# Attention by chunks of keys: the left-over keys of two pairs of heads put into one chunk

## The chip, the cores and the metric

The kernel runs on one core of a Trainium2 chip. The metric is the device time of one execution in microseconds (us), the median of three runs. Engines are named as the profile names them: PE is TensorE (PEld its weight loads), DVE is VectorE, ACT is ScalarE, SP the queue that issues most DMAs.

## What is computed

The reference is attention with a sigmoid in place of the softmax, followed by two MLPs; all of it in float32. Cut to the attention, which is the part that the change touches:

```python
# q, k, v: (2, 12, 448, 64): 2 batches, 12 heads, 448 positions, 64 wide
scores = scale * np.matmul(q, k.transpose(0, 1, 3, 2)) - np.log(S)
attn = 1.0 / (1.0 + np.exp(-scores))
out = np.matmul(attn, v)
# then: rms norm, silu(x @ w_gate) * (x @ w_val) @ w_out, and silu(h @ w_in) @ w_out
```

No weight is normalised over the keys, so the keys can be taken in any grouping and the products with v are simply added up.

## The kernel before

The 12 heads of a batch are taken in 6 pairs, so there are 12 pairs in all (`pairs`, L328). Head 0 of a pair lies on partitions 0 to 63, head 1 on 64 to 127. The 448 keys of a pair are cut into `NC` = 4 chunks of `CP` = 112.

- `prep(i)` (L344) splits the keys and queries of pair i on DVE into a high part in float32r and the rest (`ks`).
- `scores(i, c)` (L361) computes the scores of one chunk for both heads, keys on the partitions of PSUM, 448 queries along the row. Three products (high by high, low by high, high by low) are summed, each for two heads: 6 matmuls in float32r (L366), each on 64 rows of the array and 112 columns; the two heads stand on different halves of the rows and write to different banks of PSUM (`ps[:, h]`). One ACT instruction (L374) turns both heads' scores into the weights `a`. Three such PSUM tiles `sc` exist.
- `attend(i, c)` (L377) multiplies the weights by the values: one float32 matmul per head (L382) on 112 rows and 64 columns, head 0 on the left half of the columns and head 1 on the right, summed over the four chunks in one PSUM tile `av`. There are two `av` tiles, for alternate pairs.
- `collect(i)` (L390) copies a finished `av` to SBUF on DVE (L395) and squares it on ACT (L398) for the norm; both must have read it before its buffer is used again.

The order is written out by hand in the loop at L499 to L525. The 48 chunks go in 16 batches of three. One turn of the loop issues, in this order: the `collect` of the pairs that the turn before finished, the three `scores` of a batch (with `prep` of the next pair and the loads of the pair after the next two where a pair begins), the `add_square` of the collected pairs, the three `attend` of the batch before, and then what `PLAN` lists for the turn: `w` is one step of preparing the first weights of the MLPs (ACT or DVE), `n` one step of the norm of batch 0 (`norm_first`; its two float32 matmuls are L411 and L448). Each engine takes its instructions in the order in which they were issued; waits on semaphores join the engines. SP issues the loads in order too: `kq` (keys and queries, 4 buffers), `vr` (values, 5 buffers) and `raw` (weights).

After the loop the MLPs follow, with an order made by a planner (`Plan`, L65). Its matmuls (L678, L726) are in float32r on the whole array, 448 columns of data each. The change does not touch the planner or its numbers.

Of the kernel before, what the change touches and what calls it, by code (L numbers as in the profile page):

```python
# [9 lines left out]
F32 = mybir.dt.float32  # L10
F32R = mybir.dt.float32r
# [3 lines left out]
AF = mybir.ActivationFunctionType  # L15
# [3 lines left out]
B, H, S, D = 2, 12, 448, 64  # L19
NP = H // 2  # L20
DM = H * D
FF1, FF2 = 1536, 2048
P = 128
CP = 112
NC = S // CP
KD, K1, K2 = DM // P, FF1 // P, FF2 // P
SLAB = 6 * P
HALF = 3 * P
# [10 lines left out]
BUSY_A = 3.2  # L39
ZO = True  # L40
LOADED = (6, 7)
PLAN = ",,ww,ww,ww,ww,ww,ww,ww,ww,wnn,wnn,wnn,wnn,wnn,wnn,nn".split(",")
LOADS = (0, 2)
VALS = (2, 3, 4, 5)
RING = 4
# [143 lines left out]
def tile_attention_two_mlps(  # L189
# [9 lines left out]
    nc = tc.nc  # L199
# [9 lines left out]
    def ps_tile(name):  # L209
        return psum[-1].tile([P, 2, 512], F32, tag="ps", name=name)  # L210
# [41 lines left out]
    def load_next():  # L252
        load(order.pop(0))
# [4 lines left out]
    def low(dst, src, hi):  # L258
        nc.vector.tensor_tensor(dst, src, hi.bitcast(F32), ALU.subtract)  # L259
# [47 lines left out]
    def step():  # L307
        do = next(steps, None)
        if do:
            do()  # L310
# [4 lines left out]
    logs = const.tile([P, 1], F32, name="logs")  # L315
# [5 lines left out]
    with ExitStack() as actx:  # L321
        ap = actx.enter_context(tc.tile_pool(name="ap", bufs=2))
        at = actx.enter_context(tc.tile_pool(name="at", bufs=8))
        pctx = ExitStack()
        psum = [pctx.enter_context(tc.tile_pool(name="scp", bufs=3, space=PSUM))]
        avp = pctx.enter_context(tc.tile_pool(name="avp", bufs=2, space=PSUM))

        pairs = [(b, hp) for b in range(B) for hp in range(NP)]  # L328
        kq, vr, ks, att, av, acc, sqs = {}, {}, {}, {}, {}, {}, {}

        def load_pair(i):
            b, hp = pairs[i]
            kq[i] = ap.tile([P, 2, S], F32, tag="kq", name=f"kq{i}", bufs=4)
            if i:
                nc.sync.dma_start(kq[i], kqd[b, hp])
            else:
                for j, queue in enumerate((nc.sync, nc.scalar)):
                    queue.dma_start(kq[i][:, j], kqd[b, hp, :, j])

        def load_v(i):  # L340
            vr[i] = ap.tile([CP, NC, 2, D], F32, tag="vr", name=f"vr{i}", bufs=5)
            nc.sync.dma_start(vr[i], vd[pairs[i]])

        def prep(i):  # L344

            raw = kq.pop(i)
            ks[i] = kst = ap.tile([P, 2, 2, S], F32R, tag="ks", name=f"ks{i}")
            if i:
                nc.vector.tensor_copy(kst[:, 0], raw)  # L349
                nc.vector.tensor_tensor(kst[:, 1], raw, kst[:, 0].bitcast(F32), ALU.subtract)  # L350
            else:
                (hk, hq), (lk, lq) = ([kst[:, j, n] for n in range(2)] for j in range(2))
                head_, tail = slice(0, CP), slice(CP, S)
                nc.vector.tensor_copy(hk[:, head_], raw[:, 0, head_])
                low(lk[:, head_], raw[:, 0, head_], hk[:, head_])
                nc.scalar.activation(hq, raw[:, 1], AF.Copy)  # L356
                low(lq, raw[:, 1], hq)
                nc.vector.tensor_copy(hk[:, tail], raw[:, 0, tail])
                low(lk[:, tail], raw[:, 0, tail], hk[:, tail])

        def scores(i, c):  # L361
            ps = ps_tile(f"sc{i}_{c}")
            for step, (jk, jq) in enumerate(((0, 0), (1, 0), (0, 1))):
                for h in range(2):
                    rows = slice(h * D, (h + 1) * D)
                    nc.tensor.matmul(  # L366
                        ps[:CP, h, :S],
                        ks[i][rows, jk, 0, c * CP : (c + 1) * CP],
                        ks[i][rows, jq, 1, :],
                        start=(step == 0),  # L370
                        stop=(step == 2),
                    )
            a = at.tile([CP, 2, S], F32, tag="a", name=f"a{i}_{c}")
            nc.scalar.activation(a, ps[:CP, :, :S], AF.Sigmoid, bias=logs[:CP], scale=D**-0.5)  # L374
            att[i, c] = a

        def attend(i, c):  # L377
            if c == 0:
                av[i] = avp.tile([P, 512], F32, tag="av", name=f"av{i}")
            ps, a = av[i][:, :S], att.pop((i, c))  # L380
            for h in range(2):
                nc.tensor.matmul(  # L382
                    ps[h * D : (h + 1) * D],
                    vr[i][:, c, h, :],
                    a[:, h, :],
                    start=(c == 0),
                    stop=(c == NC - 1),
                )

        def collect(i):  # L390

            b, hp = pairs[i]
            ps = av.pop(i)[:, :S]
            if i < SQUARED:
                nc.vector.tensor_copy(xr[hp // 2][:, b, hp % 2], ps)  # L395
            which, home_ = ("s1", sqs) if hp else ("s0", acc)
            sq = home_[i if hp else b] = sp.tile([P, S], F32, tag=which, name=f"{which}{i}")
            nc.scalar.activation(sq, ps, AF.Square)  # L398
            if i >= SQUARED:
                nc.vector.tensor_copy(xr[hp // 2][:, b, hp % 2], ps)  # L400

        def add_square(i):

            b, hp = pairs[i]
            if hp:
                nc.vector.tensor_tensor(acc[b], acc[b], sqs.pop(i), ALU.add)

        def square_sums(b, ps):

            for c in range(NC):  # L410
                nc.tensor.matmul(  # L411
                    ps[:CP, c : c + 1], acc[b][:, c * CP : (c + 1) * CP], ones[:, 0:1], start=True, stop=True
                )

        def rsqrt(b, ps):

            home = sp.tile([P, S], F32, tag="s2", name=f"rsqrt{b}")[:CP]
            ms, y, t = (home[:, n * NC : (n + 1) * NC] for n in range(3))
            nc.vector.tensor_scalar(ms, ps[:CP, :NC], 1.0 / DM, EPS, ALU.mult, ALU.add)
            nc.vector.tensor_scalar(t.bitcast(U32), ms.bitcast(U32), 1, None, ALU.logical_shift_right)  # L420
# [3 lines left out]
            for j in range(3):  # L424
# [4 lines left out]
                nc.vector.scalar_tensor_tensor(y, t, 1.5, y, ALU.add, ALU.mult)  # L429
            diag = sp.tile([P, S], F32, tag="s3", name=f"diag{b}")[:CP].rearrange("p (c u) -> p c u", c=NC)  # L430
            nc.vector.tensor_tensor(
# [46 lines left out]
        n = len(pairs)  # L478
# [17 lines left out]
        nc.vector.memset(ones, 1.0)  # L496
        prep(0)
        turn_, ready = 0, []
        chunks = [(i, c) for i in range(n) for c in range(NC)]  # L499
        batches = [chunks[j : j + BATCH] for j in range(0, len(chunks), BATCH)]  # L500
        for before, batch in zip([[]] + batches, batches + [[]]):
            for i in ready:
                collect(i)
            for i, c in batch:
                if c == 0:
                    if i + 1 < n:
                        prep(i + 1)
                    if i + 3 < n:
                        load_pair(i + 3)
                        load_v(i + 3)  # L510
                    if i in LOADS:
                        load_next()
                scores(i, c)
            while ready:
                add_square(ready.pop(0))
            for i, c in before:
                attend(i, c)
                if c == NC - 1:
                    ready.append(i)
            for what in PLAN[turn_]:  # L520
                if what == "w":
                    step()
                else:
                    next(normal, None)
            turn_ += 1  # L525
# [20 lines left out]
    def dve(n, fn, deps=(), **more):  # L546
        return plan.add("D", 0.071 + n / 960, fn, deps, **more)
# [12 lines left out]
    def new(tag, dtype, name, n=2):  # L560
        return pools[tag[0]].tile([P, n, 2, S], dtype, tag=tag, name=name)
# [447 lines left out]
    def opened_product(n, b):  # L1009
        banks = [lambda b_=b_: opened[n](b_) for b_ in range(2)]  # L1010
        return product(banks, range(6 * n, 6 * n + 6), xs, (b,), last=b == 1)
# [4 lines left out]
    q_ = plan.add("P", 0.45, lambda: square_sums(1, sums), ready=SQUARES)  # L1016
# [39 lines left out]
    f = [Whole(f"h{p}", f"F{p}", new(f"F{p}", F32, f"h{p}")) for p in range(K1 // 2)]  # L1056
    fdone = {}
    done0 = []
    for n in range(4):
        e = opened_product(n, 1)[-1]  # L1060
# [16 lines left out]
    for p in range(1, NP1):  # L1077
# [6 lines left out]
        else:  # L1084
# [11 lines left out]
            for m in range(2):  # L1096
                e = dve(NT, lambda m=m: tt(f[1]()[:, m], pv[m](), f[1]()[:, m], ALU.mult), [ends[m]] + silu)
# [44 lines left out]
    keys = [("h", k) for k in range(6, K1)]  # L1142
# [27 lines left out]
    for p in range(NP2):  # L1170
        if p == 0:
# [3 lines left out]
            for m in range(2):  # L1175
                ps = Banks(f"i{m}", True)
                tiles = range(6 * (s + m), 6 * (s + m) + 6)
                e = product([ps.bank(b) for b in range(2)], tiles, [("y", k) for k in range(KD)], (0, 1), take="ps", start=ps.start)[-1]
# [21 lines left out]
    keys = [("g", k) for k in range(6, K2)]  # L1200
# [75 lines left out]
```

## Time and profile before

| | us |
|---|---|
| median of three runs | 541.43 (541.39 to 541.68) |
| the profiled execution, its own time | 541.37 |
| its span, first to last instruction | 539.4 |
| busy in the span: PE / PEld | 534.2 (99%) / 462.2 (86%) |
| busy in the span: DVE / ACT | 407.7 (76%) / 332.9 (62%) |

A matmul line counts one instruction; a float32 matmul leaves two records in the trace, a float32r one leaves one. Two records on different parts of the array can run at the same time, so the busy time of a line is not the sum of its durations. The chain that ended last is read from the last instruction back to the first.

### The profile page before, as it was taken

The numbers are of one execution on the slowest core, as the hardware profiler recorded it, in microseconds if no ns is written. First come the engines' busy times: TensorE is split into PE (matmuls) and PEld (weight loads), VectorE is DVE, ScalarE is ACT, GpSimd is POOL, SyncE is SP. The second block draws the span as 40 slices with busy tenths as digits, with TensorE's granted clock in tenths as the row PEclk, the third lists the DMA queues.
The fourth block names the chain that finished last, engine by engine and source line by source line (L and its number), as shares of the span: only waits on it lengthen the run. The fifth ranks groups of instructions, "written<-read, shape, count | busy, mean of one in ns | idle before, by whom it ended". The sixth has DMA issues, their size and how long they took to land.

```text
span 539.4 us, 7085 instructions
## 1 busy us (share of the span) xinstructions
PE 534.2 (99%) x2758; PEld 462.2 (86%) x2758; DVE 407.7 (76%) x637; ACT 332.9 (62%) x472; POOL 0.2 (0%) x4
## 2 busy tenths in 40 slices
PE   8999999999999999999999999999999999999997
PEld 4555459999999999999999999999999999999996
DVE  4675778998998787789797987999965994845410
ACT  6896784767787666666676535787657945224400
POOL 0000000000000000000000000000000000000000
PEclk9999999999999999999999999999999999999999
DMA  8954103313333343413542532044333336602301
GB/s 264 314 171 163 58 1 117 118 58 118 118 117 118 117 138 101 153 27 142 185 143 82 192 127 116 9 137 138 128 103 100 111 101 223 221 12 105 101 27 41
DMA packets 15521, 64.99 MB, mean 120 GB/s; under 512 B 1984, under 2 KB 3776, under 8 KB 15488
## 3 DMA queue, kind: packets, MB, share of 16 engines
q1 hardware_dynamic: 15344, 64.32, 35.9%
q8 instruction: 21, 0.34, 0.3%
q10 hardware_dynamic: 144, 0.23, 0.1%
q14 instruction: 12, 0.10, 0.1%
HBM read 61.79 MB, written 2.75 MB: 120 GB/s over the span
## 4 chain that ended last, share of the span: by engine, by line
PE 98%; DMA 1%; DVE 0%; ACT 0%; issue 0%
PE av L382 7%; PE sc L366 6%; PE v L678 5%; PE g L678 3%; PE i L678 3%; PE e1b L678 2%; PE e1a L678 2%; PE e0b L678 2%; PE e0a L678 2%; PE v2x L726 1%; PE e2x L726 1%; PE i5x L726 1%; PE o1b L678 1%; PE o0b L678 1%; PE g5x L726 1%; PE e1x L726 1%
## 5 line engine op out<-in xcount | busy, mean ns | idle before, releaser
L256 ACT ACTIVATE w<-f 128x768 fp32r<-128x768 f32 (+2 forms) x92 | 68.8, 753 | 57.9 <-PE e1b L678 7.9
L259 DVE TENSOR_TENSOR w<-f,w 128x768 fp32r<-128x768 f32 (+2 forms) x92 | 76.7, 839 | 17.8 <-ACT w L256 17.6
L266 ACT ACTIVATE f<-raw 128x768 f32<-128x768 f32 (+1 forms) x70 | 61.7, 887 | 22.9 <-DMA raw<-in_w 15.4
L278 DVE SCALAR_TENSOR_TENSOR f<-f,raw 128x768 uint32<-128x768 uint32 (+1 forms) x70 | 64.7, 931 | 6.4 <-ACT f L266 6.1
L374 ACT ACTIVATE a<-sc,logs 112x896 f32<-112x896 f32 x48 | 44.9, 1015 | 4.1 <-PE sc L366 4.0
L382 PE MATMUL av<-a,vr 112*64 112x448 f32 x192 | 39.4, 547 | 0.0
L366 PEld LDWEIGHTS sc<-ks 64*112 64x112 f32 x288 | 23.9, 171 | 14.7 <-ACT a L374 7.7
L366 PE MATMUL sc<-ks 64*112 64x448 f32 x288 | 34.0, 374 | 0.4 <-ACT ks L356 0.3
L678 PE MATMUL v<-x,w 128*128 128x448 f32 x144 | 29.9, 368 | 0.0
L382 PEld LDWEIGHTS av<-a,vr 112*64 112x64 f32 x192 | 12.4, 136 | 20.1 <-issue 19.9
L678 PEld LDWEIGHTS v<-x,w 128*128 128x128 f32 x144 | 27.0, 188 | 2.5 <-issue 0.4
L270 DVE TENSOR_SCALAR raw<-raw 128x768 uint32<-128x768 uint32 (+1 forms) x40 | 21.3, 538 | 9.6 <-DMA raw<-in_w 9.6
L274 ACT ACTIVATE raw<-raw 128x768 int32<-128x768 uint32 x30 | 26.9, 903 | 0.9 <-DMA raw<-in_w 0.9
L256 ACT ACTIVATE w<-s 128x768 fp32r<-128x768 f32 x22 | 18.5, 839 | 9.6 <-PE e1a L678 5.2
L259 DVE TENSOR_TENSOR w<-s,w 128x768 fp32r<-128x768 f32 x22 | 20.9, 950 | 3.8 <-ACT w L256 3.8
L794 ACT ACTIVATE g<-g 128x448 f32<-128x448 f32 (+1 forms) x14 | 10.7, 764 | 9.0 <-DVE g L765 9.0
L678 PE MATMUL g<-x,w 128*128 128x448 f32 x72 | 15.3, 368 | 0.0
L678 PEld LDWEIGHTS g<-x,w 128*128 128x128 f32 x72 | 13.4, 188 | 1.8 <-issue 0.7
L678 PE MATMUL i<-y,w 128*128 128x448 f32 x48 | 13.5, 365 | 0.0
L349 DVE CAST ks<-kq 128x896 fp32r<-128x896 f32 x11 | 6.9, 623 | 7.6 <-PE sc L366 5.4
L642 DVE TENSOR_TENSOR s<-s,f 128x384 f32<-128x384 f32 x22 | 12.2, 553 | 0.2
L350 DVE TENSOR_TENSOR ks<-kq,ks 128x896 fp32r<-128x896 f32 x11 | 12.0, 1092 | 0.4
(1180 smaller groups left out, 1324.1 us busy)
## 6 DMA issues: line engine op xcount, KB each, us to landing
raw<-in_w SPq DMA_DIRECT2D x58, 768.0 KB, 4.3
raw<-in_w SPq DMA_DIRECT2D x12, 640.0 KB, 3.9
kq<-in_kq SPq DMA_DIRECT2D x11, 448.0 KB, 7.3
vr<-in_v SPq DMA_DIRECT2D x12, 224.0 KB, 5.2
out_t<-e0s SPq DMA_DIRECT2D x4, 224.0 KB, 4.3
out_t<-e1s SPq DMA_DIRECT2D x4, 224.0 KB, 2.0
out_t<-e2s SPq DMA_DIRECT2D x4, 224.0 KB, 1.9
kq<-in_kq ACTq DMA_DIRECT2D x1, 224.0 KB, 3.3
```

Of the source, the lines that this page charges most:

```text
L256: nc.scalar.activation(dst, src, AF.Copy)
L259: nc.vector.tensor_tensor(dst, src, hi.bitcast(F32), ALU.subtract)
L266: nc.scalar.activation(floats[s], words(s)[:, :, 1].bitcast(F32), AF.Prelu, scale=2.0**-112, alpha=2.0**32)
L270: nc.vector.tensor_scalar(z, z, 29, None, ALU.logical_shift_right)
L274: nc.scalar.activation(z.bitcast(I32), z, AF.Copy, scale=2.0**-29 * (1 - 2.0**-18), bias=-0.5 + 2.9e-5)
L278: nc.vector.scalar_tensor_tensor(fu, fu, 3, words(s)[:, :, 0], ALU.logical_shift_left, ALU.bitwise_or)
L366: nc.tensor.matmul(ps[:CP, h, :S], ks[i][rows, jk, 0, c * CP : (c + 1) * CP], ks[i][rows, jq, 1, :], start=(step == 0), stop=(step == 2),)
L374: nc.scalar.activation(a, ps[:CP, :, :S], AF.Sigmoid, bias=logs[:CP], scale=D**-0.5)
L382: nc.tensor.matmul(ps[h * D : (h + 1) * D], vr[i][:, c, h, :], a[:, h, :], start=(c == 0), stop=(c == NC - 1),)
L642: s2 = dve(HALF, lambda: tt(sums[0][:, HALF:], sums[0][:, :HALF], block(0), ALU.subtract), [s1, m[0]])
L678: nc.tensor.matmul(banks[b](), t[:, jw], act[key](jx, b), start=(first and i == 0 and n_ == 0), stop=(final and i == n - 1 and n_ == 2), s ...
L726: nc.tensor.matmul(ps(), w[:, jw, t * P : (t + 1) * P], book[t][USES[a]][jx], start=(start and t == 0 and n == 0), stop=(stop and t == 2 a ...
```

## The change

- The keys are cut into `KC` = 3 chunks of 128 per pair, and 64 keys are left over (`KR`). The left-over keys of an even pair and of the odd pair behind it make one chunk of 128 (c == `KC`): the even pair's on partitions 0 to 63, the odd pair's on 64 to 127. There are 36 full chunks and 6 shared ones.
- A full chunk is computed as before, on 128 columns (scores) and 128 rows (values).
- The scores of a shared chunk are four float32 matmuls with the unsplit keys and queries (`kq`), one for each head and pair, on 64 rows and 64 columns. Rows are given by the head, columns by the pair. The four products with the values stand on 64 rows by the pair and 64 columns by the head, and go to the `av` tiles of both pairs.
- In a batch the shared chunk comes last among the `scores` and first among the `attend`.
- 42 chunks make 14 batches; `PLAN` spreads the same steps over 15 turns in place of 17. `kq` has 6 buffers, `ks` 3.
- On the host the values are laid out anew; an odd pair loads three chunks of them.

The diff, without the constants and the host's layout:

```diff
@@ -39,7 +41,7 @@
 BUSY_A = 3.2
 ZO = True
 LOADED = (6, 7)
-PLAN = ",,ww,ww,ww,ww,ww,ww,ww,ww,wnn,wnn,wnn,wnn,wnn,wnn,nn".split(",")
+PLAN = ",,ww,ww,ww,ww,ww,ww,wwn,wwnn,wwnn,wnn,wnn,wnn,nn".split(",")
 LOADS = (0, 2)
 VALS = (2, 3, 4, 5)
 RING = 4
@@ -330,7 +332,7 @@
 
         def load_pair(i):
             b, hp = pairs[i]
-            kq[i] = ap.tile([P, 2, S], F32, tag="kq", name=f"kq{i}", bufs=4)
+            kq[i] = ap.tile([P, 2, S], F32, tag="kq", name=f"kq{i}", bufs=6)
             if i:
                 nc.sync.dma_start(kq[i], kqd[b, hp])
             else:
@@ -338,19 +340,20 @@
                     queue.dma_start(kq[i][:, j], kqd[b, hp, :, j])
 
         def load_v(i):
-            vr[i] = ap.tile([CP, NC, 2, D], F32, tag="vr", name=f"vr{i}", bufs=5)
-            nc.sync.dma_start(vr[i], vd[pairs[i]])
+            vr[i] = ap.tile([P, KC + 1, 2, D], F32, tag="vr", name=f"vr{i}", bufs=5)
+            n = KC if i % 2 else KC + 1
+            nc.sync.dma_start(vr[i][:, :n], vd[pairs[i]][:, :n])
 
         def prep(i):
 
-            raw = kq.pop(i)
-            ks[i] = kst = ap.tile([P, 2, 2, S], F32R, tag="ks", name=f"ks{i}")
+            raw = kq[i]
+            ks[i] = kst = ap.tile([P, 2, 2, S], F32R, tag="ks", name=f"ks{i}", bufs=3)
             if i:
                 nc.vector.tensor_copy(kst[:, 0], raw)
                 nc.vector.tensor_tensor(kst[:, 1], raw, kst[:, 0].bitcast(F32), ALU.subtract)
             else:
                 (hk, hq), (lk, lq) = ([kst[:, j, n] for n in range(2)] for j in range(2))
-                head_, tail = slice(0, CP), slice(CP, S)
+                head_, tail = slice(0, P), slice(P, S)
                 nc.vector.tensor_copy(hk[:, head_], raw[:, 0, head_])
                 low(lk[:, head_], raw[:, 0, head_], hk[:, head_])
                 nc.scalar.activation(hq, raw[:, 1], AF.Copy)
@@ -359,33 +362,53 @@
                 low(lk[:, tail], raw[:, 0, tail], hk[:, tail])
 
         def scores(i, c):
+
             ps = ps_tile(f"sc{i}_{c}")
-            for step, (jk, jq) in enumerate(((0, 0), (1, 0), (0, 1))):
+            if c < KC:
+                parts = [(i, slice(0, P), slice(c * P, (c + 1) * P))]
+            else:
+                parts = [(i + e, slice(e * KR, (e + 1) * KR), slice(KC * P, S)) for e in range(2)]
+            for step, (jk, jq) in enumerate(((0, 0), (1, 0), (0, 1)) if c < KC else ((None, None),)):
                 for h in range(2):
                     rows = slice(h * D, (h + 1) * D)
+                    for n, to, keys in parts:
+                        k_, q_ = (kq[n][rows, 0], kq[n][rows, 1]) if c == KC else (ks[n][rows, jk, 0], ks[n][rows, jq, 1])
+                        nc.tensor.matmul(
+                            ps[to, h, :S],
+                            k_[:, keys],
+                            q_,
+                            start=(step == 0),
+                            stop=(step == 2 or c == KC),
+                            skip_group_check=True,
+                        )
+            a = at.tile([P, 2, S], F32, tag="a", name=f"a{i}_{c}")
+            nc.scalar.activation(a, ps[:, :, :S], AF.Sigmoid, bias=logs, scale=D**-0.5)
+            att[i, c] = a
+
+        begun = {}
+
+        def attend(i, c):
+
+            a = att.pop((i, c))
+            if c < KC:
+                parts = [(i, slice(0, P))]
+            else:
+                parts = [(i + e, slice(e * KR, (e + 1) * KR)) for e in range(2)]
+            for n, rows in parts:
+                begun[n] = begun.get(n, 0) + 1
+                if begun[n] == 1:
+                    av[n] = avp.tile([P, 512], F32, tag="av", name=f"av{n}")
+            for h in range(2):
+                for n, rows in parts:
                     nc.tensor.matmul(
-                        ps[:CP, h, :S],
-                        ks[i][rows, jk, 0, c * CP : (c + 1) * CP],
-                        ks[i][rows, jq, 1, :],
-                        start=(step == 0),
-                        stop=(step == 2),
+                        av[n][h * D : (h + 1) * D, :S],
+                        vr[i][rows, c, h, :],
+                        a[rows, h, :],
+                        start=(begun[n] == 1),
+                        stop=(begun[n] == KC + 1),
+                        skip_group_check=True,
                     )
-            a = at.tile([CP, 2, S], F32, tag="a", name=f"a{i}_{c}")
-            nc.scalar.activation(a, ps[:CP, :, :S], AF.Sigmoid, bias=logs[:CP], scale=D**-0.5)
-            att[i, c] = a
-
-        def attend(i, c):
-            if c == 0:
-                av[i] = avp.tile([P, 512], F32, tag="av", name=f"av{i}")
-            ps, a = av[i][:, :S], att.pop((i, c))
-            for h in range(2):
-                nc.tensor.matmul(
-                    ps[h * D : (h + 1) * D],
-                    vr[i][:, c, h, :],
-                    a[:, h, :],
-                    start=(c == 0),
-                    stop=(c == NC - 1),
-                )
+            return [n for n, rows in parts if begun[n] == KC + 1]
 
         def collect(i):
 
@@ -496,12 +519,14 @@
         nc.vector.memset(ones, 1.0)
         prep(0)
         turn_, ready = 0, []
-        chunks = [(i, c) for i in range(n) for c in range(NC)]
+        chunks = []
+        for i in range(0, n, 2):
+            chunks += [(i, c) for c in range(KC + 1)] + [(i + 1, c) for c in range(KC)]
         batches = [chunks[j : j + BATCH] for j in range(0, len(chunks), BATCH)]
         for before, batch in zip([[]] + batches, batches + [[]]):
             for i in ready:
                 collect(i)
-            for i, c in batch:
+            for i, c in sorted(batch, key=lambda u: u[1] == KC):
                 if c == 0:
                     if i + 1 < n:
                         prep(i + 1)
@@ -513,10 +538,8 @@
                 scores(i, c)
             while ready:
                 add_square(ready.pop(0))
-            for i, c in before:
-                attend(i, c)
-                if c == NC - 1:
-                    ready.append(i)
+            for i, c in sorted(before, key=lambda u: u[1] != KC):
+                ready += attend(i, c)
             for what in PLAN[turn_]:
                 if what == "w":
                     step()
```

Where the rows of the two programs stand, on PE. In the names, the number behind `sc` or `a` is the chunk, the last number a serial one; `ks`, `kq` and `vr` are keys and queries (split, unsplit) and values. x6 or x2 counts the same row repeated.

Second turn of the loop and the beginning of the third, before:

```order
L366 MATMUL sc_3_180<-ks_137 112x448 x6
L366 MATMUL sc_0_196<-ks_144 112x448 x6
L366 MATMUL sc_1_205<-ks_144 112x448 x6
L382 MATMUL av_214<-a_0_160,vr_125 64x448 x2
L382 MATMUL av_214<-a_1_169,vr_125 64x448 x2
L382 MATMUL av_214<-a_2_178,vr_125 64x448 x2
L366 MATMUL sc_2_221<-ks_144 112x448 x6
```

The same place now:

```order
L376 MATMUL sc_0_187<-ks_144 128x448 x6
L376 MATMUL sc_1_196<-ks_144 128x448 x6
L376 MATMUL sc_3_205<-kq_107 64x448
L376 MATMUL sc_3_205<-kq_123 64x448
L376 MATMUL sc_3_205<-kq_107 64x448
L376 MATMUL sc_3_205<-kq_123 64x448
L403 MATMUL av_212<-a_0_160,vr_125 64x448 x2
L403 MATMUL av_212<-a_1_169,vr_125 64x448 x2
L403 MATMUL av_212<-a_2_178,vr_125 64x448 x2
L376 MATMUL sc_2_219<-ks_144 128x448 x6
```

The last chunk of pair 0 has moved behind two chunks of pair 1, and six matmuls have become four that alternate between the two pairs.

From the end of the second pair (number 1) to the beginning of the fourth (number 3), which takes over its `av` buffer, before:

```order
L382 MATMUL av_259<-a_3_237,vr_127 64x448 x2
L382 MATMUL av_301<-a_0_255,vr_131 64x448 x2
L366 MATMUL sc_0_319<-ks_239 112x448 x6
L366 MATMUL sc_1_328<-ks_239 112x448 x6
L366 MATMUL sc_2_337<-ks_239 112x448 x6
L382 MATMUL av_301<-a_1_277,vr_131 64x448 x2
L382 MATMUL av_301<-a_2_286,vr_131 64x448 x2
L382 MATMUL av_301<-a_3_295,vr_131 64x448 x2
L366 MATMUL sc_3_359<-ks_239 112x448 x6
L366 MATMUL sc_0_375<-ks_312 112x448 x6
L366 MATMUL sc_1_384<-ks_312 112x448 x6
L382 MATMUL av_394<-a_0_326,vr_149 64x448 x2
```

Now:

```order
L403 MATMUL av_255<-a_2_226,vr_127 64x448 x2
L403 MATMUL av_304<-a_0_244,vr_131 64x448 x2
L403 MATMUL av_304<-a_1_253,vr_131 64x448 x2
L376 MATMUL sc_1_317<-ks_228 128x448 x6
L376 MATMUL sc_2_326<-ks_228 128x448 x6
L376 MATMUL sc_0_342<-ks_279 128x448 x6
L403 MATMUL av_304<-a_3_300,vr_131 64x448
L403 MATMUL av_352<-a_3_300,vr_131 64x448
```

Between the last product of pair 1 and the first of pair 3 stood two batches of scores and four chunks of values; now one batch of scores and two chunks of values stand there.

## Rows read from the trace of the kernel before

**Rows 1.** The page: busy time of PE, and the chain that ended last.
```profile
PE 534.2 (99%) x2758; PEld 462.2 (86%) x2758; DVE 407.7 (76%) x637; ACT 332.9 (62%) x472; POOL 0.2 (0%) x4
...
PE 98%; DMA 1%; DVE 0%; ACT 0%; issue 0%
```

**Rows 2.** The chain in order of time (start us, us, what), 0 to 100 us.
```profile
9.62 2.41 PE av L382 x12
12.03 2.02 PE sc L366 x18
14.05 2.41 PE av L382 x12
...
61.52 0.95 PE r L448 x2
...
71.30 2.03 PE sc L366 x18
73.33 4.66 PE av L382 x24
77.99 3.83 PE g L678 x18
...
86.34 0.75 PE v L448 x2
87.09 7.31 PE v L678 x36
```

**Rows 3.** Timeline of PE around one batch of values (start us, us, what, xcount).
```profile
13.28 0.77 PE L366 MATMUL sc<-ks 64*112 64x448 f32 x6
13.98 2.48 PE L382 MATMUL av<-a,vr 112*64 112x448 f32 x12
16.39 0.66 PE L366 MATMUL sc<-ks 64*112 64x448 f32 x4
```

**Rows 4.** Timeline of PE's weight loads in the same stretch.
```profile
13.98 0.20 PEld L382 LDWEIGHTS av<-a,vr 112*64 112x64 f32 x4 [0.32 <-issue]
14.41 0.14 PEld L382 LDWEIGHTS av<-a,vr 112*64 112x64 f32 x2 [0.23 <-issue]
14.79 0.14 PEld L382 LDWEIGHTS av<-a,vr 112*64 112x64 f32 x2 [0.23 <-issue]
15.16 0.14 PEld L382 LDWEIGHTS av<-a,vr 112*64 112x64 f32 x2 [0.23 <-issue]
15.54 0.14 PEld L382 LDWEIGHTS av<-a,vr 112*64 112x64 f32 x2 [0.23 <-issue]
16.39 0.47 PEld L366 LDWEIGHTS sc<-ks 64*112 64x112 f32 x6 [0.70 <-ACT a L374]
```

**Rows 5.** Windows: stretch, us, busy PE, PEld, DVE, ACT, POOL, granted clock, DMA share, GB/s.
```profile
9.62:77.99 68.37, 68.37 (x456) 34.67 (x455) 45.37 (x75) 55.14 (x70) 0.00 (x0) 1.00 0.49 157
77.99:100.00 22.01, 22.01 (x111) 20.07 (x112) 19.80 (x43) 10.45 (x15) 0.00 (x0) 1.00 0.27 89
```

**Rows 6.** Groups by line on ACT, 9.62 to 77.99 us.
```profile
L374 ACT ACTIVATE a<-sc,logs 112x896 f32<-112x896 f32 x44 | 41.2, 1016 | 2.9 <-PE sc L366 2.8
```

**Rows 7.** Timelines around two finished pairs, 19 to 24 and 31.5 to 36.2 us.
```profile
20.16 0.62 DVE L395 COPY xr<-av 128x448 f32<-128x448 f32 x1 [2.64 <-PE av L382]
...
22.12 0.90 ACT L266 ACTIVATE f<-raw 128x768 f32<-128x768 f32 x1 [1.96 <-DMA raw<-in_w]
22.92 0.53 ACT L398 ACTIVATE s<-av 128x448 f32<-128x448 f32 x1
...
32.81 0.62 DVE L395 COPY xr<-av 128x448 f32<-128x448 f32 x1
...
33.22 0.93 ACT L266 ACTIVATE f<-raw 128x768 f32<-128x768 f32 x1
34.03 0.86 ACT L256 ACTIVATE w<-f 128x768 fp32r<-128x768 f32 x1
34.77 0.56 ACT L398 ACTIVATE s<-av 128x448 f32<-128x448 f32 x1
```

More of the change, by code (lines that the diff above doesn't have):

```diff
@@ L25 @@
 NC = S // CP
+KC = S // P
+KR = S - KC * P
 KD, K1, K2 = DM // P, FF1 // P, FF2 // P
@@ L1257 @@
     w = np.ascontiguousarray(w.reshape(-1, 6, P, P).transpose(0, 2, 1, 3)).reshape(-1, P, SLAB)
+    v = v.reshape(B, NP, 2, S, D)
+    vals = np.zeros((B, NP, P, KC + 1, 2, D), np.float32)
+    vals[:, :, :, :KC] = v[:, :, :, : KC * P].reshape(B, NP, 2, KC, P, D).transpose(0, 1, 4, 3, 2, 5)
+    rest = v[:, :, :, KC * P :].transpose(0, 1, 3, 2, 4)
+    vals[:, 0::2, :KR, KC], vals[:, 0::2, KR:, KC] = rest[:, 0::2], rest[:, 1::2]
     arrays = {
         "kq": np.ascontiguousarray(np.stack([headwise(k), headwise(q)], axis=3)),
-        "v": np.ascontiguousarray(v.reshape(B, NP, 2, NC, CP, D).transpose(0, 1, 4, 3, 2, 5)),
+        "v": vals,
         "g": np.ascontiguousarray(np.asarray(inputs["moe_rms_g"]).reshape(KD, P).T),
```

## Prediction, made before the changed kernel had run

> **What bounds the kernel now.** I read the page first. PE is busy for 99% of the span, and 98% of the chain that ended last lies on it [rows 1]. The chain in order of time says how: from 9.62 to 77.99 us it is PE alone, 2.41 us of values and 2.02 us of scores in turn, 4.43 us for a batch of three chunks; the only other pieces there are the two matmul steps of the norm [rows 2]. The windows confirm it: PE is busy for 68.37 of 68.37 us at a granted clock of 1.00, while DVE has 45.4 and ACT 55.1 us of work [rows 5]. So this stage lasts as long as its matmuls, and 16 batches are 16 x 4.43 = 70.9 us.
>
> What a matmul takes must be read with care, since two of them can run at once. A float32r matmul on the whole array takes 7.31 / 36 = 0.203 us, and a float32 one, alone, leaves two records and takes 0.75, which is 0.376 a record [rows 2]. A batch of scores has 18 records; nine slots of 0.203 are 1.83 of its 2.02 us, so the two heads, on different rows of the array, run side by side. A batch of values has 12 records [rows 3], whose weight loads come in twos, 0.376 us apart [rows 4]: six slots, 2.26 of 2.41 us, two records side by side on different columns. What is left, 0.19 and 0.15 us, stands where the array's shape changes: the first values take 0.43 us to the next load instead of 0.376, and the first load of the scores stands 0.85 us behind the last load of the values [rows 4]. I put a change of shape at half of 0.34, 0.17 us. A chunk then costs 3 x 0.203 + 2 x 0.376 = 1.361 us, and 48 x 1.361 + 32 x 0.17 = 70.8: the account closes.
>
> **The change, part by part.**
>
> (a) Twelve full chunks go: -12 x 1.361 = -16.33 us.
>
> (b) Six shared chunks come, each with two steps (scores, values) of four float32 matmuls on quarters, eight records a step. No row shows a quarter. From below: a matmul's two records need the same quarter one after the other, as the lone matmul shows, so a step takes at least 0.752 us [rows 2]. From above: as halves overlap in twos both by rows and by columns [rows 2 to 4], at least two quarters overlap, and a step takes at most four slots, 1.50. I take 0.752: what two quarters share in a step (rows with different columns, columns with different rows and different banks) is what two halves share today. 12 x 0.752 = +9.02.
>
> The rows show six slots for six float32 matmuls, each with two records, so that the second record of the first matmul does not hold up the next one [rows 3, 4]. [...]
>
> (c) A shared chunk adds a change of shape to its batch of scores and one to its batch of values: 12 x 0.17 = +2.04. Ends: nothing, if quarters and halves change freely, and 0.34 each, +4.1.
>
> (d) Two batches fewer: -4 x 0.17 = -0.68.
>
> (e) Full chunks now load 128 columns. The whole-array matmuls do that already at 0.203 [rows 2], so nothing; the other end is the 3.83 us for 18 at the beginning of the MLPs, 0.213 each, which would be 36 x 3 x 0.010 = +1.1.
>
> (f) ACT loses six sigmoids of 41.2 / 44 = 0.94 us [rows 6]. They are covered by PE today, so nothing. The steps of `PLAN` and `prep` are the same and lie in a shorter stage: ACT has 55.1 - 5.6 = 49.5 us for about 62.4 (79%, today 81%), DVE 45.4 (73%, today 66%) [rows 5]. Nothing, with 13 and 17 us to spare; what spilled over would meet a DVE that is busy for 19.8 of the next 22 us, and would cost its own length.
>
> (g) SP's loads: the `kq` loads wait less with six buffers, and the second raw load no longer has the third right behind it. ACT waited 1.96 us for that raw tile without PE's noticing [rows 5, 7]. The values of an even pair are more bytes than before and those of an odd pair fewer, on average as many. Nothing; a late load would show as a wait of PE before scores or values.
>
> (h) The `av` buffers are tighter. An odd pair's buffer goes to the pair after the next, whose first product is now the shared chunk. In between lay four chunks and two batches of scores; now one or two chunks and one batch, 0.75 + 2.02 = 2.8 us at the shortest. ACT's square ended 2.5 us after the copy had begun in one place (32.81 to 35.33) and 3.3 in another (20.16 to 23.45), behind work on weights [rows 7]. So up to 0.5 us may be lost at each of four places. I take nothing; price if wrong below.
>
> Sum: -16.33 + 9.02 + 2.04 - 0.68 = -5.95 us. The MLPs keep their order, PE is busy throughout their first 22 us [rows 5], and they move forward as a whole. The profiled execution took 541.37 us, which gives 535.4; the median is 0.06 higher, so **535.5 us**. With (c) and (e) at their ends this case runs from 533.4 to 538.6; I begin at 534.0, as a change of shape that costs nothing would be unlike every one in [rows 4], and end it at 537.5.
>
> **The rivals.** A measurement here can tell about 0.2%, 1.1 us, from no change.
>
> *Two quarters at a time.* The array overlaps two matmuls, as it does in every row, and no more. A step takes 1.50 us, +9.02 on the sum: 541.4 + 3.1 = 544.5, slower. It decides from a step of 0.752 + 5.95 / 12 = 1.25 us on. For it: no row shows more than two at once. Against it: both kinds of halves work without loss.
>
> [...]
>
> *Three slots.* Two of the quarters share rows or columns in a way that holds one back; a step takes 1.13 us, +4.5: 540.0, about the edge of what can be told.
>
> *Late buffers.* Quarters overlap, but ACT's square holds PE at the four places of (h), 0.5 us each: 537.4.
>
> **How the numbers follow.** The forecast gets 0.74, as each sharing that it needs is in the rows, if not all at once; late buffers 0.06, three slots 0.07, two at a time 0.10, strict order 0.03. The point is the forecast's. The range goes from 534.0 over late buffers to the case of three slots, 540.2; it leaves out the two slow rivals (0.13) and the tails of the others. Faster by over 0.2% (below 540.35): 0.74 + 0.06 + nearly half of 0.07 = 0.83. Within 0.2%: 0.04. Slower: 0.13.
>
> **What would show it.** In the chain, the first matmul of the MLPs at about 72.1 us instead of 77.99. Batches of scores without a shared chunk stay at 2.02 us; those with one take 6 x 0.203 + 0.752 + 0.19 + 0.17 = 2.33. Batches of values take 2.41 and 2.58. The loads of a quarter step come in fours, and the next four about 0.4 us later; in twos, with four such pairs, they would show the first rival. PE's idle time before values, released by ACT's square or DVE's copy, would show late buffers. The chain after the stage should be today's, piece by piece; if its length differed by more than 0.5 us, (f) would be wrong. The prediction is wrong if a step takes over 1.25 us.

## The result, and the profile after

The changed kernel took 535.54 us, the median of four runs (535.45 to 536.36); the kernel before, run beside it, took 541.55. The ratio is 0.9892, with a 95% interval of 0.9875 to 0.9909: faster by 1.1%, where 535.5 was forecast. The profiled execution happened to be the longest of the four, 536.36 us with a span of 534.4; a second set of four runs of the same kernel, told of below, had a median of 535.52 and a profiled execution of 535.39 with a span of 533.4.

The page of the changed kernel says what [rows 1] said: PE is busy for 99% of the span and makes up 98% of the chain. There are 24 PE records fewer: 12 chunks of 10 went, and 12 steps of 8 came.

```profile
PE 529.1 (99%) x2734; PEld 458.2 (86%) x2734; DVE 407.6 (76%) x637; ACT 327.8 (61%) x466; POOL 0.2 (0%) x4
...
PE 98%; DMA 1%; DVE 0%; ACT 0%; issue 0%
...
L385 ACT ACTIVATE a<-sc,logs 128x896 f32<-128x896 f32 x42 | 39.3, 1008 | 7.8 <-PE sc L376 7.5
```

The chain in order of time of the same execution (start, us, what), beside [rows 2]:

```profile
4.85 6.05 PE sc L376 x37
10.89 2.41 PE av L403 x12
13.30 2.04 PE sc L376 x18
15.34 2.57 PE av L403 x16
17.91 2.33 PE sc L376 x20
20.24 2.40 PE av L403 x12
...
66.19 2.02 PE sc L376 x18
68.20 4.82 PE av L403 x28
73.03 3.84 PE g L701 x18
```

Batches without a shared chunk last what they did, 2.41 us of values (12 records) and 2.02 of scores (18). Those with one last 2.57 (16 records) and 2.33 (20). From the first values to the first matmul of the MLPs there is still nothing on PE that waits: the windows (columns as in [rows 5]) have it busy for all of 62.14 us, and for all of the first 22 us of the MLPs.

```profile
10.89:73.03 62.14, 62.14 (x430) 29.14 (x429) 44.32 (x74) 49.48 (x64) 0.00 (x0) 1.00 0.47 161
73.03:95.00 21.97, 21.97 (x111) 20.09 (x112) 19.11 (x42) 10.47 (x15) 0.00 (x0) 1.00 0.26 86
```

PE's weight loads (as in [rows 4]) show how the quarters run. The first row of each step holds all eight loads of the four float32 matmuls, and the next shape loads 0.91 us behind them. The records' own starts are 15.273, 15.280, 15.286 and 15.293 us for the first of each quarter: all four run at once.

```profile
15.27 0.21 PEld L403 LDWEIGHTS av<-a,vr 64*64 64x64 f32 x8 [0.31 <-issue]
16.18 0.20 PEld L403 LDWEIGHTS av<-a,vr 128*64 128x64 f32 x4 [0.70 <-issue]
...
19.26 0.21 PEld L376 LDWEIGHTS sc<-kq 64*64 64x64 f32 x8 [0.31 <-issue]
```

### The profile page after: what moved, and what is told of

Same layout as the page of the kernel before. It is cut to its first block, busy times and chain, and to the rows that moved or that the text cites. A ratio compares the mean times of both kernels' runs of the same rounds, so it can differ in the third digit from the quotient of the medians.

```text
span 534.4 us, 7022 instructions
## 1 busy us (share of the span) xinstructions
PE 529.1 (99%) x2734; PEld 458.2 (86%) x2734; DVE 407.6 (76%) x637; ACT 327.8 (61%) x466; POOL 0.2 (0%) x4
## 4 chain that ended last, share of the span: by engine, by line
PE 98%; DMA 1%; DVE 0%; ACT 0%; issue 0%
PE av L403 6%; PE sc L376 6%; PE v L701 5%; PE g L701 3%; PE i L701 3%; PE e1b L701 2%; PE e1a L701 2%; PE e0b L701 2%; PE e0a L701 2%; PE i7x L749 1%; PE i2x L749 1%; PE o2x L749 1%; PE o1b L701 1%; PE o0b L701 1%; PE v3x L749 1%; PE e1x L749 1%
## 5 line engine op out<-in xcount | busy, mean ns | idle before, releaser
L385 ACT ACTIVATE a<-sc,logs 128x896 f32<-128x896 f32 x42 | 39.3, 1008 | 7.8 <-PE sc L376 7.5
L403 PE MATMUL av<-a,vr 128*64 128x448 f32 (+1 forms) x192 | 35.4, 552 | 0.0
L376 PEld LDWEIGHTS sc<-ks 64*128 64x128 f32 x216 | 20.7, 198 | 10.7 <-ACT f L268 2.1
L403 PEld LDWEIGHTS av<-a,vr 128*64 128x64 f32 (+1 forms) x192 | 10.4, 135 | 21.3 <-issue 20.1
L376 PE MATMUL sc<-ks 64*128 64x448 f32 x216 | 27.2, 395 | 0.5 <-ACT ks L359 0.5
L418 DVE COPY xr<-av 128x448 f32<-128x448 f32 x10 | 6.2, 623 | 11.8 <-PE av L403 11.8
```

The lines of the kernel that those rows point to most:

```text
L376: nc.tensor.matmul(ps[to, h, :S], k_[:, keys], q_, start=(step == 0), stop=(step == 2 or c == KC), skip_group_check=True,)
L385: nc.scalar.activation(a, ps[:, :, :S], AF.Sigmoid, bias=logs, scale=D**-0.5)
L403: nc.tensor.matmul(av[n][h * D : (h + 1) * D, :S], vr[i][rows, c, h, :], a[rows, h, :], start=(begun[n] == 1), stop=(begun[n] == KC + 1), ...
```

## The account against the forecast

The second set is the same kernel, with no edit, and its profile starts like that of the kernel before.

> The changed kernel again, beside the next three on one chip. All theories: 535.5. The earlier profile of it had the first ten slots of scores at 0.373 us in place of 0.203, and that execution took 536.36; if this varies from one execution to the next, the times spread by up to 0.17 x 10 = 1.7 us, and a profile with fewer such slots begins its values before 10.9 us.

It took 535.52 us (535.39 to 535.59), ratio 0.9885 (0.9871 to 0.99). Its chain in order of time:

```profile
7.72 2.19 PE sc L376 x18
9.91 2.41 PE av L403 x12
12.32 2.02 PE sc L376 x18
14.34 2.57 PE av L403 x16
16.91 2.33 PE sc L376 x20
...
72.02 3.84 PE g L701 x18
```

Added up piece by piece over its chain, 14 batches of values are 3.87 us less than 16 were, and the 12 batches of scores behind the first values 2.41 less than 14. That is 6.28 from rounded rows, and the stage went from 77.99 - 9.62 = 68.37 us [rows 2, 5] to 72.02 - 9.91 = 62.11, 6.26 less. The first of the six shared batches of scores lies ahead of the first values; there the forecast's terms cost +0.752 + 0.17 - 0.609 = +0.31 us, and the values begin 0.29 later than before. Together 5.97 of the 5.98 us between the two profiled executions (541.37 and 535.39). Behind the stage nothing changed: from the first MLP matmul to the end of the span it is 461.4 us in the kernel before (539.4 - 77.99), in the first profile (534.4 - 73.03) and in the second (533.4 - 72.02), each rounded.

The first profile is 0.97 us longer because its values begin at 10.89 instead of 9.91; that is not the change's doing (last section).

## The experiments

The theory is the prediction's: four quarters run at once, a step costs 0.752 us and a change of shape 0.17, and nothing else is on the path. Each run below attacks one part of it; all are edits of the changed kernel but *the buffers alone*. In the diffs `...` stands for lines left out.

**Strict order, or not.** The full chunks' values are issued head by head, so that three matmuls of head 0 stand ahead of the first one of head 1.

```diff
-            for i, c in sorted(before, key=lambda u: u[1] != KC):
-                ready += attend(i, c)
+            for i, c in before:
+                if c == KC:
+                    ready += attend(i, c)
+            ready += attend_full([u for u in before if u[1] < KC])
...
+            for h in range(2):
+                for (i, c), a, (first_, last_) in zip(us, tiles_, flags):
```

> The changed kernel with one part of the order altered: the values of a batch's full chunks are taken head by head (all of head 0, on the left columns, then all of head 1, on the right) in place of chunk by chunk. Theory (each part of the array takes its own matmuls in order, and PE looks past one that waits for its columns): the six matmuls still fill both halves, a batch of values without a shared chunk stays at 2.41 us, the time at 535.5, within 0.5. Rival (strict order of the program): the six records of head 0 run one after the other and overlap those of head 1 at the seam alone, 11 slots of 0.376 in place of 6 (4.29 us in place of 2.41) in 8 batches, 7 in place of 4 in the other 6: 8 x 1.88 + 6 x 1.13 = +21.8, 557.3. In between: PE looks ahead over a few matmuls only.

Measured: 541.97 us (541.84 to 542.07), ratio 1.0009 (0.9999 to 1.0018). In between: the whole gain is gone, but not the 21.8 us of strict order. The chain in order of time shows where:

```profile
9.96 3.21 PE av L424 x12
13.16 2.04 PE sc L376 x18
15.21 0.91 PE av L403 x8
16.12 1.66 PE av L424 x8
```

A batch of three full chunks takes 3.21 instead of 2.41 us; 8 such batches x 0.80 = 6.4 us, all of 541.97 - 535.54. A batch with two full chunks is not longer: 0.91 + 1.66 = 2.57. The weight loads of the first batch say how:

```profile
9.88 0.19 PEld L424 LDWEIGHTS av<-a,vr 128*64 128x64 f32 x2 [0.70 <-issue]
10.31 0.14 PEld L424 LDWEIGHTS av<-a,vr 128*64 128x64 f32 x1 [0.24 <-issue]
10.69 0.19 PEld L424 LDWEIGHTS av<-a,vr 128*64 128x64 f32 x3 [0.24 <-issue]
11.06 0.19 PEld L424 LDWEIGHTS av<-a,vr 128*64 128x64 f32 x2 [0.18 <-issue]
...
16.05 0.20 PEld L424 LDWEIGHTS av<-a,vr 128*64 128x64 f32 x4 [0.70 <-issue]
```

Head 0 has six records. Head 1's first load comes at 10.69 us, when head 0's third record begins (10.687) and three of its records still wait. Where head 0 has only four records, three of them waiting, head 1 loads at once (16.05, x4). So a record does start past waiting ones in front of it: here past three of head 0's, not past four. Whole matmuls change places, too: head 1's first starts at 10.69 us, head 0's third, which was issued ahead of it, at 11.44.

**Three waiting records in all, or on each part.** If a matmul could start past three waiting records in all and no more, the four quarters could run at once only as they now stand. Here the first quarter is issued twice, so that five records wait in front of the fourth quarter.

```diff
-                    for n, to, keys in parts:
+                    for n, to, keys in (parts[:1] if c == KC and h == 0 else []) + parts:
```

> The changed kernel with the first of a shared chunk's four score matmuls issued twice (the second overwrites the first), so that in the program's order four records on one quarter stand ahead of the three other quarters. The heads-outermost run let a matmul start past three waiting records and not past four. If that limit counts all waiting records: the second quarter starts at once (three wait), the third and fourth 0.4 us later. If each quarter has a queue of its own of at least three records: all four start within 0.03 us. Either way the step takes four slots, 1.50 in place of 0.75, and the time is 535.5 + 6 x 0.752 = 540.0.

Measured, in one run: 539.93 us, which both readings expected. The loads of the step (first row: eight, as before) and the starts of the four quarters, 19.006, 19.019, 19.026 and 19.032 us, tell them apart:

```profile
19.00 0.21 PEld L376 LDWEIGHTS sc<-kq 64*64 64x64 f32 x8 [0.31 <-issue]
19.43 0.13 PEld L376 LDWEIGHTS sc<-kq 64*64 64x64 f32 x1 [0.22 <-issue]
19.81 0.13 PEld L376 LDWEIGHTS sc<-kq 64*64 64x64 f32 x1 [0.24 <-issue]
20.65 0.20 PEld L403 LDWEIGHTS av<-a,vr 128*64 128x64 f32 x4 [0.70 <-issue]
```

The fourth quarter starts 26 ns behind the first, past five waiting records, and the repeated quarter alone adds two slots. A limit of three waiting records in all is excluded; three on each part fits both runs. So does a limit, over all parts, of one whole matmul not yet begun: head 0's third matmul in the run head by head, the repeated quarter here. No run separates these two readings, and none shows a queue as such: what was measured is when records started.

**Two at a time.** The shared scores are made to run in twos, which is the first rival of the prediction made true for six of the twelve steps: the odd pair takes all 128 columns (its products on the left 64 are then overwritten), the even pair 64 behind it.

```diff
-                parts = [(i + e, slice(e * KR, (e + 1) * KR), slice(KC * P, S)) for e in range(2)]
+                parts = [(i + 1, slice(0, P), slice(S - P, S)), (i, slice(0, KR), slice(KC * P, S))]
+            if c == KC:
+                for n, to, keys in parts:
+                    for h in range(2):
...
```

> The changed kernel with the overlap of the four quarters taken away in the scores: of a shared chunk, the odd pair's two matmuls run on all 128 columns (their first 64 columns are overwritten) and then the even pair's on 64, so that only the two heads overlap. Theory (the gain is the overlap of four, and the end follows PE): a step of scores costs 4 slots in place of 2, 6 x 0.752 = +4.5, a batch of scores with a shared chunk 3.08 us in place of 2.33, the time 540.0, within 0.5. Rival (part of the gain comes from elsewhere, from fewer sigmoids or the looser buffers): the time rises by clearly less than 4.5.

Measured: 540.33 us (539.99 to 541.36), ratio 0.9978 (0.9969 to 0.9987), 4.8 us of the 6.0 gained. In the chain a shared batch of scores (two pieces) goes from 2.33 to 1.42 + 1.65 = 3.07 us, 0.74 more. Six times that is 4.4; in the profiled execution the rest lies mostly ahead of the first values, where slow slots (last section) lasted to 7.09 us:

```profile
18.16 1.42 PE sc L384 x12
19.58 1.65 PE sc L375 x8
...
76.98 3.91 PE g L709 x18
```

So the gain rests on four at once: twice those 4.4 us, for the values in twos as well, would be more than the 6.0, as the rival had it (that half was not run).

**The price of a change of shape.** The shared chunk goes between the two full ones (`middle`, left out here, puts it there), which adds one change of shape to each of 12 batches and nothing else.

```diff
...
-            for i, c in sorted(batch, key=lambda u: u[1] == KC):
+            for i, c in middle(batch):
...
-            for i, c in sorted(before, key=lambda u: u[1] != KC):
+            for i, c in middle(before):
```

> The changed kernel with the shared chunk second of the three in its batch, in the scores and in the values, which adds one change of the array's shape to each of 12 half turns and leaves the matmuls as they are. Theory (a change of shape costs 0.17 us): +2.0, 537.5, batches with a shared chunk at 2.50 (scores) and 2.74 (values). Rival (the surplus of these batches belongs to the quarters themselves, and a change of shape among full and quarter costs nothing): 535.5.

Measured: 537.58 us (537.42 to 537.60), ratio 0.9927 (0.9914 to 0.9939). (537.58 - 535.54) / 12 = 0.17 us. The chain has it for each kind: 2.72 against 2.57 us for values, 2.52 against 2.33 for scores.

```profile
14.62 2.72 PE av L403 x16
17.34 2.52 PE sc L376 x20
```

Each added change cost PE time here, 0.15 us in the values and 0.19 in the scores; what PE does in that time no row shows.

**ACT as the bound.** Each shared chunk's sigmoid is done twice, 6 x 0.94 us more of ACT, back to about its work before the change.

```diff
-            nc.scalar.activation(a, ps[:, :, :S], AF.Sigmoid, bias=logs, scale=D**-0.5)
+            for _ in range(2 if c == KC else 1):
+                nc.scalar.activation(a, ps[:, :, :S], AF.Sigmoid, bias=logs, scale=D**-0.5)
```

> The changed kernel with the sigmoid of each shared chunk computed twice, so that ACT has 48 sigmoids as before the change. Theory (ACT's work is covered by PE): 535.5, at most 0.5 more. Rival (the six sigmoids that went are part of the gain): up to 6 x 0.94 = +5.6, 541.

Measured: 535.88 us (535.68 to 536.02), ratio 0.9896 (0.9882 to 0.9909): 0.3 us for 5.6 us of work, so ACT is not on the path. The 0.3 lies in one place, the last batches of values. The chain has 5.11 us there instead of 4.82:

```profile
67.16 5.11 PE av L404 x28
```

The timeline shows why. The first loads of quarters, 0.21 us elsewhere, last 0.50 here, and ACT's square of the earlier pair, pushed back by the doubled sigmoid, ends at 67.33 in the middle of them:

```profile
66.79 0.54 ACT L422 ACTIVATE s<-av 128x448 f32<-128x448 f32 x1 [0.76 <-DVE xr L419]
67.09 0.50 PEld L404 LDWEIGHTS av<-a,vr 64*64 64x64 f32 x8 [0.31 <-issue]
```

In the changed kernel itself the same place has room: its square ends at 67.41 us, 0.72 ahead of the loads.

```profile
66.86 0.55 ACT L421 ACTIVATE s<-av 128x448 f32<-128x448 f32 x1 [0.82 <-DVE xr L418]
...
68.13 0.21 PEld L403 LDWEIGHTS av<-a,vr 64*64 64x64 f32 x8 [0.31 <-issue]
```

**The buffers alone.** The kernel before, with the change's six `kq` and three `ks` buffers.

```diff
-            kq[i] = ap.tile([P, 2, S], F32, tag="kq", name=f"kq{i}", bufs=4)
+            kq[i] = ap.tile([P, 2, S], F32, tag="kq", name=f"kq{i}", bufs=6)
...
-            ks[i] = kst = ap.tile([P, 2, 2, S], F32R, tag="ks", name=f"ks{i}")
+            ks[i] = kst = ap.tile([P, 2, 2, S], F32R, tag="ks", name=f"ks{i}", bufs=3)
```

> The kernel before with nothing of the change but the buffers: six for keys and queries in place of four, three for their split form in place of two. Theory (PE never waited for these): 541.5, within 0.3. Rival (part of the gain is the looser loads): up to 1 us faster.

Measured: 541.34 us (541.12 to 542.42), ratio 0.999 (0.9971 to 1.0009), so no change that can be told. The interval alone would leave room for 1.6 us; the chain does not. From the first values to the first MLP matmul it is 68.36 us (78.38 - 10.02), where the kernel before had 68.37 (77.99 - 9.62), so no part of the 6.26 us gained there is the buffers'.

```profile
10.02 2.41 PE av L382 x12
...
78.38 3.83 PE g L678 x18
```

**The slow first slots.** In the first profile the first ten slots of scores last until 8.74 us, the first of them 0.53 us and the others 0.373 each. PE had waited for 0.53 us just before:

```profile
4.85 5.13 PE L376 MATMUL sc<-ks 64*128 64x448 f32 x30 [0.53 <-ACT ks L359]
```

The idle matmuls on zeros keep PE busy while the first loads come, from 1.15 to 4.32 us in that profile. Two more of them close this gap.

```diff
-IDLE = 8
+IDLE = 10
```

> The changed kernel with 10 matmuls on zeros ahead of the first scores in place of 8, which fills the 0.53 us in which PE waited for the first keys. Theory (PE runs its first scores slowly because it had stood still before them): the first scores start at most 0.2 us later, all their slots take 0.203, 534.8 to 535.5. Rival (the slow slots come whatever PE did before, or end at a fixed time): 535.5 or up to 0.4 more, since the first scores start later.

Measured: 535.83 us, ratio 0.989 (0.9875 to 0.9904). The theory of this run, that the gap makes the slots slow, fell: PE went from the idle matmuls into the scores without one, and the first slots of scores (all but the very first, 0.53) took 0.373 us all the same, until 6.65 us. Its chain in order of time:

```profile
1.15 3.92 PE idle L510 x10
5.07 3.42 PE sc L376 x23
```

## Why the prediction was right

- **(a)** and **(d)** were right: unchanged batches kept 2.41 and 2.02 us, and the pieces of the stage add up to the forecast's sum within 0.02 us.
- **(b)** was the disputed term, and its lower bound held: four quarters at once, 0.91 us from a step to the next shape, which is 0.752 and one change of shape. *Two quarters at a time* and *three slots* are excluded by the four starts within 20 ns and by the 0.91 us, and the run in twos shows what the first of them would have cost in the scores. *Strict order*, which has 0.03 among the chances, would have PE start its matmuls as they were issued. No run shows it: in the run head by head a matmul started 0.75 us ahead of one issued before it, and the time was 541.97 us, not 557.3. The reading under (b) was right, yet less general than it sounded: in that run a matmul passed three waiting records and not four. The shared chunk, with three waiting records to pass on the way to its fourth quarter, one in each other part, is within what was seen to work. One sign was stated wrongly: the loads of a step were to come in fours, the next four 0.4 us later, and came as eight at once. The first row of [rows 4] has it already: four loads for two float32 matmuls, both records of each.
- **(c)** was right: 0.17 us on the mean, from 12 added changes in a run of their own. The forecast had halved 0.34 for two of them; the two measured, 0.15 for values and 0.19 for scores, are the remainders that it had read one by one.
- **(e)** was right at nothing: 18 records on 128 columns take 2.02 us, as on 112.
- **(f)** was right: ACT has 49.48 us of work in 62.14, as worked out, and DVE 44.32. Even with the sigmoids put back only one place shows.
- **(g)** was right: PE waits twice in the first 100 us, 1.1 us for DVE before the idle matmuls and 0.5 for ACT before the first scores, and never directly for a load; and the MLP part is unchanged to 0.1 us.
- **(h)** came out at nothing, in part by luck: the forecast's own rows allowed up to 0.5 us at each of four places, and the closest place had 0.72 us to spare. *Late buffers* did not come; the run with doubled sigmoids shows it in one place, 0.3 us, so the mechanism is real and the spare time small.

The shared batches were forecast at 2.33 and 2.58 us and took 2.33 and 2.57; the first MLP matmul at 72.1 and came at 72.02 in the second profile. What the forecast didn't name is that one of the six shared batches of scores lies ahead of the first values. The sum isn't changed by it, only where it shows: 0.29 us there, 6.26 in the stage. Nor did it allow for a first stretch that varies from one execution to the next by as much as 1 us.

## What to carry to other kernels

Where PE is the bound, count slots of the array, not matmuls: four float32 matmuls on 64 rows and 64 columns cost one matmul's time here (0.91 us with a change of shape of about 0.17, where one alone took 0.75), and a left-over that would have filled a part of the array alone can share it with that of another problem. Issue the parts in turn: three matmuls of one part ahead of the other cost 0.80 us a batch. Put steps of one shape together, since each change cost 0.17 us. By an estimate some 40 of them, 6.8 us, are left in this stage (two for each of 14 batches and 12 for the shared chunks). A batch is held to three chunks by the three PSUM tiles of scores, and longer batches were not tried.

## What the runs showed of the hardware

- **Matmuls started past waiting ones of other parts of the array.** The run head by head lets the other half start past three waiting records and not past four, and the run with the first quarter twice lets the fourth start past five, no more than three of them in one part. Head 1's first matmul starts 0.75 us ahead of head 0's third, which was issued before it (10.69 and 11.44 us). So what is said of each engine ahead of the prediction, that it takes its instructions in the order of issue, does not hold for PE's matmuls on different parts here. On one part no row shows a matmul ahead of an earlier one, and the two records of a lone float32 matmul follow each other (0.75 us for both [rows 2]). How PE does this no run shows, and other types were not tried.
- **The first scores were slower in some profiles.** A slot of 448 columns took 0.373 us there, and so did the idle matmuls ahead of them (0.373 us from each start to the next but for the first, in the kernel before and in the first profile of the changed one); behind them a slot is 0.203. The clock column shows nothing of it, for a window over slow slots reads 1.00:

```profile
6.80:8.80 2.00, 2.00 (x14) 1.76 (x14) 1.36 (x2) 1.78 (x3) 0.00 (x0) 1.00 1.05 393
```

But the trace has no clock record for that window: its first one, of the full clock, starts only at 8.85 us in this profile, in the slot from 8.74 to 9.00, the first that is shorter. In the run with ten idle matmuls it starts at 6.75, where the slots of 0.373 had lasted to 6.65. In the second profile of the changed kernel (4.37) and in that of the kernel before (4.25) it starts ahead of the first scores, and neither has slow slots. Over the ten profiles it lies between 4.25 and 8.85 us, with PE's idle matmuls beginning at 1.15 in each. The kernel before with other buffers has it at 7.10 and slots of 0.373 until 6.86, so it comes without the change, too. A gap of PE ahead of the scores is not the cause either: the record starts early in the two profiles with gaps of 0.32 and 0.33 us, and late in the one without a gap. What clock was granted ahead of that record no trace shows, and what sets the moment stays open. Of the 0.97 us that the first profile is longer, 0.22 lie ahead of its first scores (they start at 4.85 and not 4.63) and the rest between these and the first values, where the slow slots are.
